# One weight read in full rows, in the last head group of the last pass

## The chip, the cores and the metric

The kernel runs on one core of one Trainium2 chip. Its time is device microseconds of one execution. Before the change the median of three runs is 1935.85 us (1933.0 to 1936.69). One further execution was profiled.

The engines are named as in the profile: PE multiplies matrices, DVE (VectorE) and ACT (ScalarE) work on vectors, POOL issues the stores, SP issues the loads.

## The reference

Forward and backward pass of four layers for one token: attention, feed-forward, attention, feed-forward, where both attention layers share the weights wq and wo and the K and V caches, and both feed-forward layers share w1 and w2.

```python
def _A_ref(x, k_cache, v_cache, wq, wo):
    q = (x @ wq).reshape(B, Sq, Hq, Dh).transpose(0, 2, 1, 3)
    k = jnp.repeat(k_cache, rep, axis=1)
    v = jnp.repeat(v_cache, rep, axis=1)
    scores = jnp.einsum("bhqd,bhkd->bhqk", q, k) * (Dh ** -0.5)
    p = _softmax(scores, axis=-1)
    o = jnp.einsum("bhqk,bhkd->bhqd", p, v)
    return o.transpose(0, 2, 1, 3).reshape(B, Sq, Hq * Dh) @ wo
...
x = x + _A_ref(_layernorm(x, axis=-1), A_k_cache, A_v_cache, A_wq, A_wo)
x = x + _B_ref(_layernorm(x, axis=-1), B_w1, B_b1, B_w2, B_b2)
x = x + _A_ref(_layernorm(x, axis=-1), A_k_cache, A_v_cache, A_wq, A_wo)
x = x + _B_ref(_layernorm(x, axis=-1), B_w1, B_b1, B_w2, B_b2)
```

The outputs are the result and the gradients of the input x, both caches, wq, wo, w1, b1, w2 and b2. The model width is 1024; there are 32 query heads of 128 columns, four K/V head groups (eight query heads each) and 65536 cached positions, all in bf16. A cache is 67 MB, wq is 1024 x 4096 (8 MB).

What the change touches is the gradient of the first layer's normalised input, which needs wq times the gradient of the queries: for each of the 1024 rows of wq, a sum over all 4096 columns of wq times dq. One head group owns 1024 of these columns.

## The kernel before, in words

The kernel passes four times over the caches. The last pass (`attn_bwd4`, called at L2024) does the backward of both attention layers at once: it reads K and V and writes dK and dV. It takes the four head groups one after another, and within a group 64 items of eight 128-position chunks each. Four items are a block: one load of K (1 MB), one of V, one store of dK and one of dV.

**Steps.** `pipeline` (L846) runs over steps; in each step every stage (`vT`, `vS`, `eT`, `dV8`, `xT`, `dK8`, `k8`) handles one item, each with its own lag. After the stages of a step, `bg.step` lets the background work go on by one piece. `Background` (L783) has an urgent list, whose first generator is asked in each step and uses up the step unless it yields "wait"; otherwise the normal list may do one piece, when it is behind an even share (L803). `bg.drain` (L826) runs all that is left. The last pass stands under no order written by hand: a scheduler arranges the instructions of each engine, and each engine then works strictly in that order.

**Memory slots.** An arena of 20 slots of 8 KB per partition (1 MB each) holds loaded blocks and outgoing blocks. In the last pass (`take_one`, L298) the free slots are of two kinds: those in the set RING, for outgoing blocks (`fill=True`), and the others, for loads. Either kind gives its oldest slot first. RING begins with up to five slots, and as each group ends, the two slots that held its softmax weights join it (`E_done`, L903). A slot is free for its next user once the program has issued its last use; the engine that uses it next waits until that use, or that store, has finished. All loads stand in SP's queue in one order, all stores in POOL's.

**The wq work.** When the last block of a group is done, `on4` (L1997) adds two pieces of background: `g_dn` (L998), urgent, for the product with the group's columns of wq, and `gwq` (L1994), normal, for the outer products that make this group's columns of the wq gradient (out_4). `g_dn` loads the group's 1024 columns in two loads of 1 MB (`wq_slabs`, L483: rows of 2 KB, four 128-row chunks each), the second when the first is used up, into load slots. It spreads the group's dq over all partitions (`g_bcast_vec`, L556), and for each of the eight row chunks DVE multiplies (L595) and ACT sums up along the row (L584). The last group is done apart: two loads of 1 MB 20 steps before the end (`pre_load`), eight chunks turned by PE (L688) and kept turned (`Rows`, L609) in `fill4` ten steps before the end, and then, when the last dq is there, one matrix product each (L722). `Rows()` takes two slots for the turned chunks (L619).

In `fill4` the rest of the normal background is drained; `g_outer_last` (L1515) then makes the last group's outer products.

Of the kernel before, what the change touches and what calls it, by code (L numbers as in the profile page):

```python
# [10 lines left out]
BF = mybir.dt.bfloat16  # L11
F32 = mybir.dt.float32
ACTF = mybir.ActivationFunctionType
ALU = mybir.AluOpType
AX = mybir.AxisListType
PSUM = bass.MemoryType.PSUM
P = 128
# [3 lines left out]
def kernel(  # L21
# [24 lines left out]
    nc = tc.nc  # L46
    D = A_x.shape[-1]
    G = A_k_cache.shape[1]
# [3 lines left out]
    HQ = QD // DH  # L52
    R = HQ // G
    F = B_w1.shape[1]
    DC, FC = D // P, F // P
# [19 lines left out]
    vec = ctx.enter_context(tc.tile_pool(name="vec", bufs=1))  # L75
    tmp = ctx.enter_context(tc.tile_pool(name="tmp", bufs=2))
    ktpool = ctx.enter_context(tc.tile_pool(name="ktpool", bufs=4))
    mvs = ctx.enter_context(tc.tile_pool(name="mvs", bufs=2))
# [15 lines left out]
    def ps_gg():  # L94
        return PS["pool"].tile([P, 1024], F32, name="ps_gg", tag="gg", bufs=2)
# [4 lines left out]
    def ps_mv(shape, dtype=F32):  # L100
        if PS["pass4"]:
            return ps_tr(shape, dtype)
        return PS["pool"].tile(shape, dtype, name="ps_mv", tag="mv", bufs=1)
# [5 lines left out]
    ident_f = const.tile([P, P], F32, name="ident_f")  # L109
    make_identity(nc, ident_f[:])  # L110
    ident_b = const.tile([P, P], BF, name="ident_b")
# [28 lines left out]
    load = {"act": 0.0, "dve": 0.0, "pe": 0.0}  # L140
# [4 lines left out]
    def add_load(act=0.0, dve=0.0, pe=0.0):  # L145
        load["act"] += act
        load["dve"] += dve
        load["pe"] += pe

    def evac(out, in_, kind="bf"):  # L150
        n = 1
        for d in in_.shape[1:]:
            n *= d
        ca = 0.17 + n * 0.00083
        cd = 0.13 + n * (0.00105 if kind == "f32" else 0.00054)

        if PS["pass4"] and kind == "bf":
            ca += 1.5
        if kind == "kta" or kind != "kt" and load["act"] + ca <= load["dve"] + cd:
            load["act"] += 0.17 + n * 0.00083  # L160
            nc.scalar.copy(out=out, in_=in_)  # L161
        else:
            load["dve"] += cd
            nc.vector.tensor_copy(out=out, in_=in_)  # L164
# [243 lines left out]
    B4_LAG = DK_LAG + J // 8  # L408
    DV_LAG = TLEAD + 1
    V_LEAD = 4 * J // 8  # L410
    ITEMS = [order_by_unit(False, SU), order_by_unit(True, SU), order_by_unit(False, HB), order_by_unit(True, J)]
# [23 lines left out]
    def rows_of(W):  # L435
        return W.rearrange("(kc p) n -> p kc n", p=P)
# [1 line left out]
    def f_rows_of(W):  # L438
        return W.rearrange("(s p j) n -> p s j n", p=P, j=4)

    def slabs(name, load, nk, kper, ncols, ahead=1, flat=False):
        pend = deque()
        ks = deque(range(0, nk, kper))

        def fetch():
            k = ks.popleft()
            i = None
            if ks and flat and NOW["wide"] and not odd_one():
                i = take_pair()
            if i is None:  # L450
                kn = min(kper, nk - k)
                sl = Slot(name)
            else:
                kn = min(2 * kper, nk - k)
                ks.popleft()
                sl = Slot(name, at=i, both=True)
            v = sl.t[:, 0:kn * ncols].rearrange("p (k n) -> p k n", n=ncols)
            nc.sync.dma_start(out=v, in_=load(k, kn))
            pend.append((k, kn, sl, v))

        def gen():
            while ks or pend:
                while ks and len(pend) < ahead:
                    fetch()
                k, kn, sl, v = pend.popleft()
                for kk in range(kn):
                    NOW["slab"] = sl
                    yield k + kk, v[:, kk, :]
                sl.over = True
                if not sl.users:  # L470
                    sl.free()
        g = gen()
        g_fetch = [fetch for _ in range(ahead)]
        return g, g_fetch
# [8 lines left out]
    def wq_slabs(g, ahead=1):  # L483
        v = rows_of(A_wq)
        return slabs("s_wq", lambda k, kn: v[:, k:k + kn, g * 1024:(g + 1) * 1024], DC, 4, 1024, ahead, True)
# [88 lines left out]
    def g_rowdots(slab_it, nk, vcol, nj, finish, name):  # L574
        n = nj * P
        y = vec.tile([P, nk], F32, name=name)
        nc.gpsimd.memset(y[:], 0.0)
        vbc = None
        due = None
        steps = 8 if PS["pass4"] else WAIT_STEPS  # L580

        def total(t, kc):
            def f():
                nc.scalar.activation(out=t[:, :], in_=t[:, :], func=ACTF.Copy, accum_out=y[:, kc:kc + 1])  # L584
            return f
        for kc, slab in slab_it:
            if vbc is None:
                vbc = yield from g_bcast_vec(vcol, nj)
                for _ in range(steps - WAIT_STEPS + 1):
                    yield "wait"  # L590
            elif kc % 4 == 0:
                for _ in range(steps):
                    yield "wait"
            t = mvs.tile([P, n], BF, name="mv_t", tag="mv_t", bufs=2)
            nc.vector.tensor_tensor(out=t[:, :], in0=slab, in1=vbc[:, :], op=ALU.mult)  # L595
            add_load(dve=0.1 + n * 0.00054, act=0.42 + n * 0.00083)
            if due is not None:
                due()
            due = total(t, kc)
            yield  # L600
        due()
        yield
        r = finish(y[:, :])
        if r is not None:
            yield from r
        yield


    class Rows:  # L609
        def __init__(self, pool=None, bufs=NWT):  # L610
            self.pool, self.bufs = pool, bufs
            self.views = deque()
            self.n = 0
            self.made = 0
            self.parts = 0
            if pool is None:

                for _ in range(2):
                    t = Slot("s_wt").t[:, :].rearrange("p (v a b) -> p v a b", v=4, a=8)  # L619
                    self.views.extend(t[:, v, :, :] for v in range(4))  # L620
                self.bufs = 8
            self.queue = deque()
            self.jobs = deque()
            self.feed = None
# [290 lines left out]
    def gsl(g):  # L915
        return slice(g * R, (g + 1) * R)
# [73 lines left out]
    def dn_finish(dn, first):  # L990
        def fin(y):
            if first:
                nc.vector.tensor_copy(out=dn[:], in_=y)
            else:
                nc.vector.tensor_tensor(out=dn[:], in0=dn[:], in1=y, op=ALU.add)
        return fin

    def g_dn(L, dn, g, first):  # L998
        yield from g_rowdots(wq_slabs(g)[0], DC, L["dqT"][:, gsl(g)], R, dn_finish(dn, first), "%s_dn%d" % (L["name"], g))


    ACT_KT = (3, 13, 15)
# [591 lines left out]
    L1, L3 = new_layer("L1", 0), new_layer("L3", 1)  # L1594
# [31 lines left out]
    lastg = [ITEMS[p][-1][0] for p in range(4)]  # L1626
    firstg = [ITEMS[p][0][0] for p in range(4)]
    PRE = {}

    def pre_load(key, pair):  # L1630
        def f():
            PRE[key] = prefetch(pair())
        return f

    gxbc = bcast_vec(gx[:], DC)
    bg = Background()
# [18 lines left out]
    rows = Rows(DENSE["pool"])  # L1655
# [20 lines left out]
    bg = Background()  # L1676
# [86 lines left out]
    rows = Rows(DENSE["pool"])  # L1763
    wo3b = wo_slabs(firstg[2])
    eps4 = root_ready(L3, lastg[1])
    ahead = [0]
# [17 lines left out]
    with tc.manual_schedule(engines=ORDERED):  # L1784
# [28 lines left out]
        job = rows.job(R, DC, lambda: dx3[:], dO_finish(L3, firstg[2]))  # L1813
# [28 lines left out]
    bg = Background()  # L1842
# [17 lines left out]
    rows = Rows(DENSE["pool"])  # L1860
# [110 lines left out]
    b4 = ExitStack()  # L1971
# [22 lines left out]
    def gwq(g):  # L1994
        return g_outer(bgpool, out_4, DC, R, [L3["n"], L1["n"]], [L3["dqT"][:, gsl(g)], L1["dqT"][:, gsl(g)]], c0=g * 1024)

    def on4(g):  # L1997
        if g != lastg[3]:
            bg.add(g_dn(L1, dn1, g, g == firstg[3]))
            bg.normal.append(gwq(g))  # L2000
        else:
            next(PRE["gwq"])
            PRE["rows"].run()
            next(PRE["gwq"])
            dxn1 = ln_bwd(dn1[:], L1["n"], L1["rstd"])
            dx0 = tmp.tile([P, DC], F32, name="dx0")
            nc.vector.tensor_tensor(out=dx0[:], in0=dx1[:], in1=dxn1[:], op=ALU.add)
            col_to_dram(dx0, D, out_1.rearrange("a b d -> (a b d)"))
            run(PRE["gwq"])
# [4 lines left out]
            kv8("v", g, c8)  # L2014

    def fill4():
        PRE["rows"] = Rows()
        PRE["rows"].add(PRE["wq4"], DC, R, lambda: L1["dqT"][:, gsl(lastg[3])], dn_finish(dn1, False))
        PRE["rows"].fill()
        bg.drain()  # L2020
        PRE["gwq"] = g_outer_last(bgpool, out_4, [L3["n"], L1["n"]], [L3["dqT"][:, gsl(lastg[3])], L1["dqT"][:, gsl(lastg[3])]],
                                  lastg[3] * 1024)
        next(PRE["gwq"])
    attn_bwd4(3, L1, L3, on4, bg, b4, [(12 + B4_LAG, last_v), (20, pre_load("wq4", lambda: wq_slabs(lastg[3], 2))), (10, fill4)])  # L2024
    b4.close()
    ps4_stack.close()

# [29 lines left out]
```

## Time and profile before

| what | value |
|---|---|
| time, median of three runs | 1935.85 us |
| profiled execution: time, span | 1936.17 us, 1934.3 us |
| DMA: moved, mean rate over the span | 787.62 MB, 407 GB/s |
| busy share of the span: PE, DVE, ACT | 81%, 61%, 54% |
| loads in the last pass: K, V, wq (1 MB each) | 64, 57, 8 |
| stores of 1 MB in the last pass | 149 |

The span runs from the first to the last instruction of the profile; the time has 1.87 us more around it. The DMA row of the page gives the busy share of the 16 DMA engines in 40 slices of 48.4 us; the last pass fills slices 25 to 40. A line with several stages gives, for each stretch, the busy time of each engine with the number of instructions, then the granted clock of PE, the DMA share and the rate. A bracket behind an instruction tells how long its engine stood idle before it, and what it waited for; a DMA wait that the profile could not place is written "issue".

### The profile page before, as it was taken

The numbers are of one execution on the slowest core, as the hardware profiler recorded it, in microseconds if no ns is written. First come the engines' busy times: TensorE is split into PE (matmuls) and PEld (weight loads), VectorE is DVE, ScalarE is ACT, GpSimd is POOL, SyncE is SP. The second block draws the span as 40 slices with busy tenths as digits, with TensorE's granted clock in tenths as the row PEclk, the third lists the DMA queues.
The fourth block names the chain that finished last, engine by engine and source line by source line (L and its number), as shares of the span: only waits on it lengthen the run. The fifth ranks groups of instructions, "written<-read, shape, count | busy, mean of one in ns | idle before, by whom it ended". The sixth has DMA issues, their size and how long they took to land. (4 is left out here: it accounts for less than half of the span.)

```text
span 1934.3 us, 66768 instructions
## 1 busy us (share of the span) xinstructions
PE 1576.4 (81%) x30099; PEld 1292.1 (67%) x30099; DVE 1172.2 (61%) x2448; ACT 1043.8 (54%) x1619; POOL 142.4 (7%) x325
## 2 busy tenths in 40 slices
PE   6878778678878878978787878888996987787977
PEld 6878777678777878867677875555654554454544
DVE  5645555255555554645464576777876886676766
ACT  3434334245333535446363465766876785576765
POOL 0000000000000000000000002111211211121211
PEclk9989999799999988998999999898988998798997
DMA  9999999999999999999999997999999999899998
GB/s 393 427 427 424 429 428 416 399 420 412 428 425 428 428 422 330 379 425 429 426 420 426 405 348 298 425 420 387 424 424 413 420 425 423 349 423 397 425 422 321
DMA packets 107148, 787.62 MB, mean 407 GB/s; under 512 B 9440, under 2 KB 16622, under 8 KB 42222
## 3 DMA queue, kind: packets, MB, share of 16 engines
q1 hardware_dynamic: 82782, 617.65, 77.3%
q0 software_dynamic: 24080, 165.70, 20.5%
q8 instruction: 235, 3.85, 0.7%
q14 instruction: 51, 0.42, 0.1%
HBM read 617.62 MB, written 165.69 MB: 405 GB/s over the span
## 5 line engine op out<-in xcount | busy, mean ns | idle before, releaser
L164 DVE COPY kt<-ps_tr 128x1024 bf16<-128x1024 bf16 x736 | 505.8, 688 | 427.1 <-PE ps_tr L1030 239.5
L161 ACT CAST arena<-ps_gg 128x1024 bf16<-128x1024 f32 x457 | 444.2, 1011 | 183.2 <-PE ps_gg L1434 132.4
L1030 PE MATMUL ps_tr<-ident_b,arena 128*128 128x128 bf16 x3840 | 308.4, 225 | 48.0 <-DMA arena<-in_A_k_cache_dram 35.3
L161 ACT COPY kt<-ps_tr 128x1024 bf16<-128x1024 bf16 x180 | 188.6, 1054 | 184.5 <-PE ps_tr L1224 107.2
L164 DVE CAST arena<-ps_gg 128x1024 bf16<-128x1024 f32 (+2 forms) x186 | 222.4, 1196 | 80.1 <-PE ps_gg L1434 36.0
L1030 PEld LDWEIGHTS <-arena 128*128 128x128 bf16 x3840 | 231.8, 101 | 56.7 <-DMA arena<-in_A_k_cache_dram 37.8
L1434 PE MATMUL ps_gg<-GG,xt 64*128 64x512 bf16 x1024 | 209.8, 408 | 51.2 <-DVE arena L164 36.7
L1131 PE MATMUL ps_acc<-arena 128*128 128x64 bf16 (+4 forms) x4096 | 204.6, 197 | 46.1 <-DMA arena<-in_A_v_cache_dram 33.7
L1048 PE MATMUL ps_sc<-L_qpad,kt 128*128 128x64 bf16 (+7 forms) x3584 | 182.6, 194 | 23.1 <-issue 11.7
L1353 PE MATMUL ps_tr<-ident_b,arena 128*128 128x128 bf16 x1824 | 178.1, 232 | 28.5 <-DMA arena<-in_A_v_cache_dram 25.7
L1113 ACT ACTIVATE arena<-S_sb,L_negm 128x128 bf16<-128x128 f32 x256 | 165.3, 1006 | 57.2 <-DVE L_negm L1098 43.6
L1224 PE MATMUL ps_tr<-ident_b,arena 128*128 128x128 bf16 x2032 | 161.7, 224 | 40.6 <-DMA arena<-in_A_v_cache_dram 39.1
L1131 PEld LDWEIGHTS <-arena 128*128 128x128 bf16 x4096 | 160.0, 101 | 52.1 <-DMA arena<-in_A_v_cache_dram 37.7
L1353 PEld LDWEIGHTS <-arena 128*128 128x128 bf16 x1824 | 117.6, 103 | 84.7 <-issue 54.2
L1048 PEld LDWEIGHTS <-kt 128*128 128x128 bf16 x3584 | 152.0, 100 | 27.3 <-issue 12.8
L1224 PEld LDWEIGHTS <-arena 128*128 128x128 bf16 x2032 | 122.6, 100 | 46.0 <-DMA arena<-in_A_v_cache_dram 41.7
L1465 PEld LDWEIGHTS <-arena 128*128 128x128 bf16 x2048 | 92.4, 101 | 56.4 <-issue 38.5
L1434 PEld LDWEIGHTS <-xt 64*128 64x128 bf16 x1024 | 64.4, 94 | 97.8 <-issue 60.2
L1113 ACT ACTIVATION_READ_ACCUMULATOR arena<-S_sb,L_negm 128x1 f32 x256 | 128.2, 501 | 0.0
L584 ACT ACTIVATE mv_t<-mv_t 128x1024 bf16<-128x1024 bf16 x96 | 102.0, 1064 | 43.0 <-DVE mv_t L595 42.8
L1278 PE MATMUL ps_acc<-dsT,arena 128*128 128x64 bf16 (+7 forms) x2048 | 102.4, 194 | 12.4 <-DMA arena<-in_A_k_cache_dram 7.2
L1390 PE MATMUL ps_sc<-DOB,kt 128*128 128x64 bf16 (+3 forms) x1824 | 112.3, 197 | 0.1
(319 smaller groups left out, 2104.3 us busy)
## 6 DMA issues: line engine op xcount, KB each, us to landing
arena<-in_A_k_cache_dram SPq DMA_DIRECT2D x82, 2048.0 KB, 21.3
arena<-in_A_v_cache_dram SPq DMA_DIRECT2D x79, 2048.0 KB, 20.1
out_dram<-arena POOLq DMA_DIRECT2D x149, 1024.0 KB, 15.6
arena<-in_A_v_cache_dram SPq DMA_DIRECT2D x84, 1024.0 KB, 13.1
arena<-in_A_k_cache_dram SPq DMA_DIRECT2D x84, 1024.0 KB, 14.6
arena<-in_A_wo_dram SPq DMA_DIRECT2D x22, 1024.0 KB, 14.9
arena<-in_B_w_dram SPq DMA_DIRECT2D x21, 1024.0 KB, 10.0
arena<-in_A_wq_dram SPq DMA_DIRECT2D x18, 1024.0 KB, 13.4
```

The lines of the kernel that those rows point to most:

```text
L161: nc.scalar.copy(out=out, in_=in_)
L164: nc.vector.tensor_copy(out=out, in_=in_)
L584: nc.scalar.activation(out=t[:, :], in_=t[:, :], func=ACTF.Copy, accum_out=y[:, kc:kc + 1])
L1030: nc.tensor.transpose(pt[:, i, :], kb8[:, i, :], ident_b[:, :])
L1048: nc.tensor.matmul(state["ps_s"][:, s:s + w, :].rearrange("p a b -> p (a b)"), lhsT=kt[:, i, :], rhs=L["qpad"][:, g, 0:w, :].rearrange("p ...
L1113: nc.scalar.activation(out=E(p, g, c0, SU)[:, :, h], in_=S[:, h, :], func=ACTF.Exp, bias=L["negm"][:, g, su, h:h + 1], scale=SCALE, accum_ ...
L1131: nc.tensor.matmul(ps_o[:, 0:w, :], lhsT=vb8[:, i, :], rhs=E(p, g, c, w), start=(c % SU == 0), stop=(c % SU == SU - 1), skip_group_check=True)
L1224: nc.tensor.transpose(pt[:, i, :], vb8[:, i, :], ident_b[:, :])
L1278: nc.tensor.matmul(ps_dq[:, 0:w, :].rearrange("p a b -> p (a b)"), lhsT=kb8[:, i, :], rhs=dsT[:, s:s + w, :].rearrange("p a b -> p (a b)") ...
L1353: nc.tensor.transpose(pt[:, i, :], vb8[:, i, :], ident_b[:, :])
L1390: nc.tensor.matmul(state["ps_dp"][:, s:s + w, :].rearrange("p a b -> p (a b)"), lhsT=vt[:, i, :], rhs=DOB[:, g, 0:w, :].rearrange("p a b - ...
L1434: nc.tensor.matmul(pg[:, 512 * h:512 * h + 512], lhsT=xt[64 * h:64 * h + 64, j1 // 8 + m, :], rhs=gg[64 * h:64 * h + 64, :, :].rearrange(" ...
```

## The change

wq is no longer read group by group in the second, third and last group's time. One generator, `g_dn_rows`, is added to the urgent background when the third group to be worked on is done, that is, at the beginning of the last group. It reads wq in eight loads of 1 MB, each 128 full rows of 8 KB. For each of these it multiplies and sums the columns of the three finished groups (three products on DVE, three sums on ACT), and has PE turn the columns of the last group, which are kept turned until the last dq is there. After each slab it lets two steps pass. The slabs, the spread dq of three groups and the two slots for turned chunks are taken from RING (the new argument `ring` of `slabs`, and `Slot("s_wt", True)`); a slab is fetched when the one before the previous one is used up. `fill4` no longer loads or turns anything.

```diff
-    def slabs(name, load, nk, kper, ncols, ahead=1, flat=False):
+    def slabs(name, load, nk, kper, ncols, ahead=1, flat=False, ring=False):
...
-                sl = Slot(name)
+                sl = Slot(name, ring)
...
-                    t = Slot("s_wt").t[:, :].rearrange("p (v a b) -> p v a b", v=4, a=8)
+                    t = Slot("s_wt", True).t[:, :].rearrange("p (v a b) -> p v a b", v=4, a=8)
...
+    def g_dn_rows(L, dn, last, rows, job):
+        rest = (G - 1) * R
+        lo = 0 if last else 1
+        v = rows_of(A_wq)
+        it, fetch = slabs("s_wq", lambda k, kn: v[:, k:k + kn, :], DC, 1, HQ * P, 2, False, True)
+        fetch[0]()
+        vsl = Slot("wq_vbc", True)
+        vb = vsl.t[:, 0:rest * P]
+        pt = ps_mv([rest, P], F32)
+        nc.tensor.transpose(pt[:, :], L["dqT"][:, lo * R:lo * R + rest], ident_f[:, :])
+        vr = tmp.tile([32, P], BF, name="bc_rows")
+        nc.vector.tensor_copy(out=vr[0:rest, :], in_=pt[:, :])
+        yield
+        for j0 in range(0, rest, 4):
+            pg = ps_gg()
+            for jj in range(4):
+                nc.tensor.matmul(pg[:, jj * P:(jj + 1) * P], lhsT=ident_b[0:rest, j0 + jj:j0 + jj + 1].to_broadcast([rest, P]),
+                                 rhs=vr[0:rest, :], start=True, stop=True)
+            evac(vb[:, j0 * P:(j0 + 4) * P], pg[:, 0:512], kind="f32")
+            if j0 % 8:
+                yield
+        y = vec.tile([P, DC, G - 1], F32, name=L["name"] + "_dny")
+        nc.gpsimd.memset(y[:, :, :], 0.0)
+        due = None
...
+        for kc, slab in it:
+            for n in range(G - 1):
+                t = mvs.tile([P, R * P], BF, name="mv_t", tag="mv_t", bufs=2)
+                nc.vector.tensor_tensor(out=t[:, :], in0=slab[:, (lo * R + n * R) * P:(lo * R + n * R + R) * P],
+                                        in1=vb[:, n * R * P:(n + 1) * R * P], op=ALU.mult)
+                add_load(dve=0.1 + R * P * 0.00054, act=0.42 + R * P * 0.00083)
+                if due is not None:
+                    due()
+                due = total(t, kc, n)
+                yield
+            rows.tra(job, kc, slab[:, last * R * P:(last + 1) * R * P], 0)
+            yield
+            if kc < DC - 1:
+                yield "wait"
+                yield "wait"
+        due()
+        yield
+        nc.vector.tensor_reduce(out=dn[:], in_=y[:, :, :], axis=AX.X, op=ALU.add)
+        vsl.free()
+        yield
...
+    beforeg = ITEMS[3][2 * len(ITEMS[3]) // G][0]
+
     def on4(g):
         if g != lastg[3]:
-            bg.add(g_dn(L1, dn1, g, g == firstg[3]))
             bg.normal.append(gwq(g))
+            if g == beforeg:
+                PRE["rows"] = Rows()
+                job = PRE["rows"].job(DC, R, lambda: L1["dqT"][:, gsl(lastg[3])], dn_finish(dn1, False))
+                bg.add(g_dn_rows(L1, dn1, lastg[3], PRE["rows"], job))
...
     def fill4():
-        PRE["rows"] = Rows()
-        PRE["rows"].add(PRE["wq4"], DC, R, lambda: L1["dqT"][:, gsl(lastg[3])], dn_finish(dn1, False))
-        PRE["rows"].fill()
         bg.drain()
...
-    attn_bwd4(3, L1, L3, on4, bg, b4, [(12 + B4_LAG, last_v), (20, pre_load("wq4", lambda: wq_slabs(lastg[3], 2))), (10, fill4)])
+    attn_bwd4(3, L1, L3, on4, bg, b4, [(12 + B4_LAG, last_v), (10, fill4)])
```

`total` (left out above) returns the ACT sum of one product; it is issued behind the next product.

More of the change, by code (lines that the diff above doesn't have):

```diff
@@ L999, in g_dn, with total, f @@
         yield from g_rowdots(wq_slabs(g)[0], DC, L["dqT"][:, gsl(g)], R, dn_finish(dn, first), "%s_dn%d" % (L["name"], g))
+    def g_dn_rows(L, dn, last, rows, job):
[22 more added lines that the diff above has]
+        due = None
+        def total(t, kc, n):
+            def f():
+                nc.scalar.activation(out=t[:, :], in_=t[:, :], func=ACTF.Copy, accum_out=y[:, kc, n:n + 1])
+            return f
+        for kc, slab in it:
[18 more added lines that the diff above has]
+        yield
     ACT_KT = (3, 13, 15)
```

## The prediction, made before the changed kernel was run

> **What bounds the kernel now.** I read the summary of the page first, then stretches of the last pass (10 us each), then what ended the idle time of VectorE (DVE), then how long transfers take from issue to landing.
>
> ```profile
> span 1934.3 us, 66768 instructions
> ...
> DMA  9999999999999999999999997999999999899998
> ```
>
> The reader sees a kernel that moves bytes: the DMA row holds 9s from end to end. In the last pass (about 1195 us to the end) a full stretch moves 422 to 428 GB/s; I use 424. What can be won there is time in which the DMA engines fall idle. The stretches (columns: busy time of PE, PE loads, DVE, ACT, POOL with counts, granted clock, DMA share, GB/s) show where:
>
> ```profile
> 1470.00:1480.00 10.00, 1.36 (x23) 1.09 (x20) 1.27 (x3) 1.23 (x3) 0.44 (x2) 0.71 1.02 425
> ...
> 1490.00:1500.00 10.00, 8.86 (x139) 6.00 (x135) 9.32 (x21) 9.52 (x14) 1.70 (x4) 1.00 0.94 355
> ...
> 1650.00:1660.00 10.00, 5.98 (x88) 3.84 (x86) 3.56 (x6) 5.01 (x7) 1.06 (x2) 0.93 1.02 419
> 1660.00:1670.00 10.00, 0.00 (x0) 0.00 (x0) 1.80 (x3) 1.08 (x3) 0.00 (x0) 0.50 0.66 277
> 1670.00:1680.00 10.00, 9.92 (x103) 6.42 (x103) 7.00 (x13) 6.66 (x11) 2.15 (x5) 0.55 0.71 269
> 1680.00:1690.00 10.00, 9.84 (x136) 6.55 (x138) 9.39 (x18) 8.58 (x10) 1.09 (x2) 1.00 0.99 367
> ...
> 1770.00:1780.00 10.00, 7.00 (x72) 4.77 (x71) 6.98 (x12) 6.45 (x9) 1.07 (x2) 0.60 0.87 305
> ```
>
> Against 424 GB/s the four rows around 1495 and 1660 to 1690 lose 1.6 + 3.5 + 3.7 + 1.3 = 10.1 us, and the row at 1770 loses 2.8 us; 1470 to 1480 loses nothing although all engines stand still. The DVE rows name the cause:
>
> ```profile
> 1478.73 0.69 DVE L595 TENSOR_TENSOR mv_t<-arena,vbc 128x1024 bf16<-128x1024 bf16 x1 [10.22 <-DMA arena<-in_A_wq_dram]
> ...
> 1668.20 0.69 DVE L595 TENSOR_TENSOR mv_t<-arena,vbc 128x1024 bf16<-128x1024 bf16 x1 [14.40 <-issue]
> ...
> 1771.05 0.69 DVE L595 TENSOR_TENSOR mv_t<-arena,vbc 128x1024 bf16<-128x1024 bf16 x1 [12.99 <-issue]
> ```
>
> L595 is the product of a wq slab in the background work of a finished head group. DVE works in order, so a late slab stops it, and PE behind it (idle 9.7, 13.6 and 12.2 us at the same places). All three are second halves of a group's wq: issued by SP at 1448.65, 1649.64 and 1750.06, used 30.1, 18.6 and 21.0 us later. Landing times over the last pass (last column, us), and below them those right after the long stall:
>
> ```profile
> out_dram<-arena POOLq DMA_DIRECT2D x149, 1024.0 KB, 15.6
> arena<-in_A_k_cache_dram SPq DMA_DIRECT2D x64, 1024.0 KB, 15.4
> arena<-in_A_v_cache_dram SPq DMA_DIRECT2D x57, 1024.0 KB, 11.7
> arena<-in_A_wq_dram SPq DMA_DIRECT2D x8, 1024.0 KB, 23.4
> ```
>
> ```profile
> out_dram<-arena POOLq DMA_DIRECT2D x3, 1024.0 KB, 6.0
> arena<-in_A_k_cache_dram SPq DMA_DIRECT2D x2, 1024.0 KB, 5.0
> ```
>
> So a 1 MB transfer takes 5 to 6 us when the queues have run dry and 12 to 23 us when they are full.
>
> ```profile
> 1885.00:1897.00 12.00, 11.92 (x98) 6.59 (x99) 6.92 (x9) 5.13 (x6) 0.53 (x1) 0.50 0.96 399
> ```
>
> After a stall of 9.5 us the granted clock is 0.50 for 12 us: 98 matmuls, where 1700 to 1730 does 132 per 10 us.
>
> **The change part by part.** The sum is made against the profiled execution: span 1934.3 us, 1936.17 us with what lies around it (1.9); the median shown is 1935.85, 0.3 below it.
>
> *Removed in the second and third group.* Four 1 MB wq loads, 16 products on DVE (0.68 us each) and 16 sums on ACT (1.06 + 0.20 us) leave the stretch 1415 to 1685. The bytes come back later, so they win nothing; the idle time caused by the two waits goes: -10.1 us. What is late next there is K and V (PE waited 10.0 us for V at 1621 with the DMA share at 1.01: no loss). The wait at 1771 in the last group belongs to a load that no longer exists: -2.8 us, replaced below. Sum -12.9 us.
>
> *Row length.* wq now comes in 8 KB rows instead of 2 KB. The 10 us stretches with a wq load move 417 to 420 GB/s, about 5 below the rest, 0.12 us per load, eight loads: -1.0 us (ends 0 and -1.5).
>
> *Work that only moves.* Products stay 24, sums 24, the transposed broadcast 24 matmuls and six evictions: 0 in total. Sixteen products and sums now fall into the last group (11 us of DVE, 20 of ACT over 10.5 blocks). Cover: DVE and ACT are 70 to 80% busy there while DMA is at 1.01; in exchange the outer products (two L161/L164 evictions in six steps instead of four) are pushed back. I cost it at 0; with the cover gone it is 31 us less about 11 pushed-back evictions of 1.1 us, shared by two engines: 9.5 us.
>
> *Added: a chain for each wq row slab.* Before, a wq slab took a load slot, free once PE had read it. Now it takes a ring slot, and SP must wait until the store that left this slot has landed. So each slab costs store landing + load landing between the issue of that store and the first product on DVE. How much work lies between comes from the order in which the built program stands: about 305 instructions of all engines a block of four items, and a block takes 10.5 us where nothing stalls (spacing of the L1411 products at 1819 to 1872), so 0.0344 us each. From store to first product the eight slabs have 936, 877, 659, 466, 348, 325, 404, 346 instructions = 32.2, 30.2, 22.7, 16.0, 12.0, 11.2, 13.9, 11.9 us. The method can be tried on the kernel before: the slot of the slab used at 1668 came free 161 instructions (5.5 us) ahead, the load took 18.6, which gives a wait of 13.1 (seen: 14.40); at 1771: 289 instructions, 9.9 us, 21.0, so 11.1 (seen: 12.99).
> The landing pair is bounded by the rows above: dry 6.0 + 5.0 = 11.0; full 15.6 + 13.5 (mean of K and V, whose row length wq now has) = 29.1. Each stall lets queues run down, so neither end lasts: I take the middle, 10.8 + 9.3 = 20.1. Waits of the eight: 0, 0, 0, 4.1, 8.1, 8.9, 6.2, 8.2 = 35.5 us. Part of it the transfers need anyway: slabs stand 386 instructions (13.3 us) apart, 1.26 blocks, which move 5.3 MB of K, V, dK, dV, 1.05 of wq and 0.3 of outer products = 6.7 MB, 15.7 us at 424; 2.4 us for each of five = 12.0. Net +23.5 us. At the dry end the net is 0; at the full end the waits are 86.9 less 14.4 = +72.5. The half clock after each stall shortens the next wait by as much as it slows the work between, so it adds 0 (the end above: 5 x 3.6 us, from 98 matmuls in 12 us against 132 in 10).
>
> *What queues behind the added wait.* On SP, 2, 4, 3, 4, 2, 3 and 3 K and V loads stand between the row loads and are held with them. Their slots now come free 9 to 12 steps ahead instead of mostly 5 to 9, since wq leaves the load slots: 0; without that cover a K load late as at 1885 costs 9.5 us. On POOL three out_4 stores stand ahead of the last two out_2 stores.
>
> *The end.* The urgent work takes 52 steps of the last group, so 12 units of outer products are left to the drain, where 1 was: eight more evictions (1.0 to 1.2 us) and three row builds (1.9) = 14.6 us over two engines, +7.3. The turning of the last wq (eight evictions, 6.2 us) leaves the end: -3.1. K loads, no longer kept out by four wq slots, are not late at 1876 to 1885, which saves the idle DMA of the half-clock stretch: -2.0. Sum +2.2. The 2 MB of later stores (4.9 us) fit into a share of 0.7 after 1915.
>
> Sum: 1934.3 - 12.9 - 1.0 + 23.5 + 2.2 = 1946.1; + 1.9 = 1948.0 for this execution, 1947.7 against the median.
>
> *Two pages beside it.* The Trainium skill, "TensorE: Matmul & The Clock Gate" (Part 1: The HAM clock gate), has the array at half rate after an idle window of about 3.4 us, until some 3.4 us of sustained work. The trace agrees on the half, not on the way back: 12 us. By the page five stalls would cost 5 x 1.7 = 8.5 us where the rows give 18, and the sum takes neither.
>
> **The rivals.**
> 1. *The chain runs dry (faster).* If store and load land in 6.0 and 5.0 us, 11.0 is below all eight distances, no product waits, and only the gains stay: 1934.3 - 12.9 - 1.0 + 2.2 = 1922.6, 1924.2 with the surroundings. For it: the landing times at 1655 to 1690. Against: these followed a 14.4 us stall; at 1800 to 1880 a store took 23.2 us. It decides below a pair of about 13 us.
> The Trainium skill, "DMA: Bandwidth & Descriptors" (Queues, rings and completion order), says that each DMA engine takes turns between the queues that have work, so a store need not stand behind the loads; that speaks for this rival. No run here shows the turns.
> 2. *It cancels.* With a pair of 16 us the last five waits are 0, 4.0, 4.8, 2.1 and 4.1 = 15.0, less 2.4 for each of four: +5.4. With half of the lost cover (4.8) that is 1924.2 + 10.2 - 0.3 = 1934.1, within 0.2%. For and against it: the same two landing times, between which it lies.
> 3. *The chain stays full (much slower).* +72.5: 1997. Against: in that case DMA would be a third idle, and idle queues are not full.
>
> **How the numbers follow.** Forecast (slower by the chain) 0.54, its own range 1940 to 1980; rival 1 0.28; rival 2 0.14; rival 3 0.04. 0.2% is 3.9 us, about what can be told from no change. Faster 0.28, same 0.14, slower 0.58. Leaving out one in ten on each side, the range goes from below rival 1 to inside the full end: 1919 to 1978.
>
> **What the profile after would show.** Right: no DVE idle over 5 us on a wq product before about 1700; the last group's first block ahead by 10 to 20 us; then four to six DVE idles of 4 to 10 us before the row products (L1033), with SP waiting at L458 on out_dram, the clock at 0.5 to 0.8 and DMA share at 0.8 to 0.95. Wrong: row products that never wait (rival 1), or idle DMA in the second and third group in spite of the missing loads, or an end from block 64 that is longer by over 5 us.

## The result, and the profile after

The changed kernel takes 1955.0 us (median) against 1936.0 us for the kernel before: ratio 1.0097, 95% interval 1.0080 to 1.0114. It is slower, as forecast (1947.7, range 1919 to 1978), by 19 us where 11.8 were forecast. The profiled execution has a span of 1953.8 us (before 1934.3).

The summary of the page shows no change of kind: DMA stays the row of 9s, with a weaker last digit.

```profile
span 1953.8 us, 66829 instructions
...
DMA  9999999999999999999999988999999999999995
```

The 10 us stretches of the last pass, to be read against those of before (columns: busy time of PE, PE loads, DVE, ACT, POOL with counts, granted clock, DMA share, GB/s):

```profile
1490.00:1500.00 10.00, 9.71 (x126) 5.94 (x123) 8.08 (x11) 7.91 (x10) 2.29 (x4) 1.00 1.02 423
1660.00:1670.00 10.00, 7.78 (x101) 4.88 (x99) 4.99 (x9) 7.01 (x8) 1.78 (x5) 1.00 1.02 426
1670.00:1680.00 10.00, 8.53 (x86) 4.86 (x85) 6.55 (x9) 5.06 (x5) 1.43 (x3) 0.66 1.01 425
1680.00:1690.00 10.00, 9.15 (x132) 5.86 (x131) 7.11 (x13) 6.89 (x7) 1.93 (x4) 1.00 1.02 420
1780.00:1790.00 10.00, 8.57 (x106) 5.51 (x104) 6.23 (x10) 7.05 (x10) 1.07 (x2) 0.84 1.00 376
1810.00:1820.00 10.00, 1.85 (x13) 1.09 (x13) 4.33 (x7) 3.61 (x6) 0.00 (x0) 0.51 0.89 348
1870.00:1880.00 10.00, 7.68 (x79) 4.65 (x78) 8.00 (x15) 6.91 (x9) 0.53 (x1) 0.58 0.67 282
1920.00:1930.00 10.00, 8.13 (x98) 5.09 (x99) 7.46 (x28) 5.25 (x7) 0.98 (x2) 0.81 0.52 211
1930.00:1940.00 10.00, 6.70 (x35) 1.84 (x33) 6.17 (x13) 5.58 (x7) 2.35 (x4) 0.50 0.59 247
```

The first four stretches, which moved 355, 277, 269 and 367 GB/s before, are full now: the idle DMA of the second and third group is gone. The others are what replaced it: 282 to 376 GB/s in the last group, and a long end in which the engines move 211 to 247 GB/s and PE falls to half clock (0.81, then 0.50).

To count this I use one ledger for every kernel below: in each stretch of 10 us, the time lost against 424 GB/s is 10 x (1 - GB/s / 424); the losses are added up between fixed times. All kernels but one move the same bytes, so the difference of two spans is the difference of their losses. The ledger is good to some 3 us: from 1190 to 1410 us, where the kernels stand in the same order, it gives between 5.1 and 11.4 us.

```
loss of DMA time (us)    1410-1690   1690-1900   1900-end   span
before                      10.3         5.3         9.8    1934.3
after                        0.3        25.1        20.7    1953.8
```

So the second and third group won 10.0 us, the last group lost 19.8, the end lost 10.9 (the stretch ahead of them, which the change does not touch, differs by 1.7). For the last group, the idle times of DVE ahead of the row products:

```profile
1776.13 0.69 DVE L1033 TENSOR_TENSOR mv_t<-arena 128x1024 bf16<-128x1024 bf16 x1 [8.84 <-DMA arena<-in_A_wq_dram]
...
1815.67 1.29 DVE L1033 TENSOR_TENSOR mv_t<-arena 128x1024 bf16<-128x1024 bf16 x2 [9.83 <-DMA arena<-in_A_wq_dram]
...
1870.97 0.69 DVE L1033 TENSOR_TENSOR mv_t<-arena 128x1024 bf16<-128x1024 bf16 x1 [11.24 <-DMA arena<-in_A_wq_dram]
```

and sums over 1690 to 1900 us (us in total, times, longest), first DVE's wait for a row slab, then what SP's queue stood for:

```profile
DVE mv_t L1033 <- DMA arena<-in_A_wq_dram: 36.6, 6, 11.2
```

```profile
SPq L458 <- DMA out_dram<-arena: 99.2, 8, 22.8
SPq L361 <- PE ps_acc L1515: 59.6, 7, 15.2
```

The 36.6 us over six slabs are what the forecast called 35.5 over five. SP stands 99.2 us before its eight row loads (L458), each time because the ring slot that it is to fill is still being stored. What that does to the queue shows in SP's own rows (start us, us):

```profile
1703.51 0.33 SPq L361 DMA_DIRECT2D arena<-in_A_k_cache_dram  x1
1726.92 0.33 SPq L458 DMA_DIRECT2D arena<-in_A_wq_dram  x1
1727.35 0.51 SPq L361 DMA_DIRECT2D arena<-in_A_k_cache_dram  x1
1727.95 1.14 SPq L361 DMA_DIRECT2D arena<-in_A_v_cache_dram  x1
```

From 1703.5 to 1726.9 no load is issued at all; the K and V loads follow the row load at once, so they had only stood behind it.

### The profile page after: what moved, and what is told of

The parts are those of the page before. It is cut to its first block, busy times and chain, and to the rows that moved or that the text cites. A ratio compares the mean times of both kernels' runs of the same rounds, so it can differ in the third digit from the quotient of the medians.

```text
span 1953.8 us, 66829 instructions
## 1 busy us (share of the span) xinstructions
PE 1594.9 (82%) x30097; PEld 1303.2 (67%) x30097; DVE 1172.0 (60%) x2444; ACT 1045.0 (53%) x1619; POOL 142.7 (7%) x323
## 5 line engine op out<-in xcount | busy, mean ns | idle before, releaser
L161 ACT CAST arena<-ps_gg 128x1024 bf16<-128x1024 f32 (+1 forms) x460 | 447.5, 1009 | 194.1 <-PE ps_gg L1484 118.2
L1098 PE MATMUL ps_sc<-L_qpad,kt 128*128 128x64 bf16 (+7 forms) x3584 | 182.6, 194 | 21.1 <-issue 9.9
L1098 PEld LDWEIGHTS <-kt 128*128 128x128 bf16 x3584 | 151.9, 100 | 25.4 <-issue 11.3
L1274 PEld LDWEIGHTS <-arena 128*128 128x128 bf16 x2032 | 124.8, 102 | 42.5 <-DMA arena<-in_A_v_cache_dram 37.6
L1440 PEld LDWEIGHTS <-kt 128*128 128x128 bf16 x1824 | 83.3, 102 | 39.2 <-issue 38.0
## 6 DMA issues: line engine op xcount, KB each, us to landing
arena<-in_A_k_cache_dram SPq DMA_DIRECT2D x82, 2048.0 KB, 20.8
arena<-in_A_v_cache_dram SPq DMA_DIRECT2D x79, 2048.0 KB, 21.1
arena<-in_B_w_dram SPq DMA_DIRECT2D x21, 1024.0 KB, 10.1
arena<-in_A_wq_dram SPq DMA_DIRECT2D x18, 1024.0 KB, 10.9
```

What stands on the lines that cost most here:

```text
L1098: nc.tensor.matmul(state["ps_s"][:, s:s + w, :].rearrange("p a b -> p (a b)"), lhsT=kt[:, i, :], rhs=L["qpad"][:, g, 0:w, :].rearrange("p ...
L1274: nc.tensor.transpose(pt[:, i, :], vb8[:, i, :], ident_b[:, :])
L1440: nc.tensor.matmul(state["ps_dp"][:, s:s + w, :].rearrange("p a b -> p (a b)"), lhsT=vt[:, i, :], rhs=DOB[:, g, 0:w, :].rearrange("p a b - ...
```

## The experiments

The theory on record: the row slabs cost what they cost because a ring slot must wait for its store, then for its load, and DVE, PE and ACT stand in order behind the late slab. Rivals: long rows that cost the transfers themselves; the row work itself; the end. Each kernel is timed beside the kernel before, and ratios are to it. "The end" is the time from the last X product on DVE (block 64) to the last instruction: 31.1 us before, 41.4 after.

**Slots without a store in the chain (own3).**

```
+ own = deque(Slot("s_wq", True) for _ in range(3))
- slabs("s_wq", ..., DC, 1, HQ * P, 2, False, True)
+ slabs("s_wq", ..., DC, 1, HQ * P, 3, False, True, own)   # fetch: sl = own[0]; own.rotate(-1)
```

> Changed kernel, but the eight row slabs go in turn through three slots that they keep to themselves (taken from the ring once, given back after the last slab), three slabs ahead. From the second round on no slab waits for a store. Chain theory (a slab's slot waits for the store that left it): the three DVE idles of 8.8, 9.8 and 11.2 us before L1033 go, SP stands at L458 on out_dram for under 40 us in all (99.2 in the changed kernel), and the time falls by 20 to 25 us to 1930 to 1936. Rival, rows of 8 KB cost the transfers themselves: loads stay above 42 us of DMA-engine time per MB in the last group (38 elsewhere) and the time stays at 1950 to 1956. In both cases the stretch from block 64 to the end stays near 41 us, since 12 units are still left to the drain.

Measured: ratio 1.0068 (1.0047 to 1.0088), 1950.9 us; the end 42.7 us. SP's waits in 1690 to 1900 us, and what PE waited for at the broadcast:

```profile
SPq L361 <- PE ps_acc L1520: 105.5, 12, 16.1
...
SPq L460 <- PE ps_tr L690: 28.8, 4, 14.8
SPq L460 <- DMA out_dram<-arena: 25.2, 3, 20.8
```

```profile
1737.12 0.58 PE L1020 MATMUL ps_gg<-bc_rows,ident_b 24*128 24x128 bf16 x4 [10.55 <-ACT arena L161]
```

The stand for stores fell from 99.2 to 25.2 us as expected, but DVE still waits 26.5 us for row slabs (36.6 before the edit). In place of the store SP now stands for K's slots, which PE frees (105.5 us, 59.6 in the changed kernel). That stand is no cost in itself, for the kernel before has the same in these 210 us, at nearly the full rate:

```profile
SPq L361 <- PE ps_acc L1465: 105.3, 13, 13.0
```

New are 28.8 us for its own three slots, which PE still turns, with the other loads behind; a row load issued at 1758.4 was used 26.6 us later. A new wait came as well: the slot of the broadcast vector (`wq_vbc`) is taken from the ring after the three slabs, its store had not landed, and PE, behind ACT's eviction into it, stood 10.6 us. My theory predicted 1930 to 1936 and fails in this form: with three quarters of the stand for stores gone, the slabs are still late. (The 4 us are hardly more than the two intervals leave open.) The time is inside what the rival of long rows had forecast (1950 to 1956); that rival is taken up under loadshare.

**More lead, same slots (ahead3).**

```
- slabs("s_wq", ..., DC, 1, HQ * P, 2, False, True)
+ slabs("s_wq", ..., DC, 1, HQ * P, 3, False, True)
```

> Changed kernel, with three row slabs ahead instead of two, ring slots as they come. Each load is issued about 13 us earlier in the order, but its slot still waits for a store. If the cost is DVE's wait for the late slab, the waits before L1033 fall below 2 us each and the time goes to 1935 to 1940. If the cost is SP standing still for the store's landing, with the K and V loads behind it, SP still stands for 80 to 110 us on out_dram, PE waits for K or V instead, and the time stays within 5 us of 1955.

Measured: 1.0054 (1.0035 to 1.0074), 1947.7 us, between the two forecasts.

```profile
SPq L458 <- DMA out_dram<-arena: 91.3, 8, 20.3
```

```profile
DVE mv_t L1033 <- DMA arena<-in_A_wq_dram: 28.7, 3, 11.4
```

SP stands almost as long, and DVE waits 28.7 us in three waits instead of 36.6 in six. The loss in 1690 to 1830 us is the same (16.1 against 15.8), and falls from 9.3 to 3.7 in 1830 to 1900. A third slab in flight helps late, not where the waits begin.

**Outer products beside the row work (share).**

```
                 due = total(t, kc, n)
-                yield
+                yield "wait"
             rows.tra(job, kc, slab[:, last * R * P:(last + 1) * R * P], 0)
-            yield
+            yield "wait"
```

> Changed kernel, but each step of the row work lets one step of the outer products run beside it (the plain yields become waits), so that they are no longer pushed to the drain. If the long end (41 us from block 64, 31 in the kernel before) comes from the 12 units left to the drain: it falls to 31 to 34 us and the time to 1945 to 1949, the waits before L1033 staying. If the end is long for other reasons, or the units cost as much wherever they are: 1952 to 1958.

Measured: 1.0054 (1.0035 to 1.0073), 1947.8 us. The end falls by 12.8 us, from 41.4 to 28.6; block 64 comes 5.6 us later (1918.0 against 1912.4), which leaves 7.2. After block 64 there are 14 evictions from `ps_gg` into slots and three row builds fewer (17 and three against 31 and six). The long end was the outer products that the row work had pushed to the drain. This shows why they cost so much there; ACT's and PE's rows in the end of the changed kernel (start, us, idle before and what ended it):

```profile
1941.33 1.01 ACT L161 CAST arena<-ps_gg 128x1024 bf16<-128x1024 f32 x1 [0.71 <-PE ps_gg L1562]
1943.05 1.01 ACT L161 CAST arena<-ps_gg 128x1024 bf16<-128x1024 f32 x1 [0.70 <-PE ps_gg L1562]
```

```profile
1943.25 0.62 PE L1562 MATMUL ps_gg<-rowb,rowa 2*128 2x512 bf16 x2 [0.24 <-DVE arena L164]
1944.11 0.62 PE L1562 MATMUL ps_gg<-rowb,rowa 2*128 2x512 bf16 x2 [0.24 <-ACT arena L161]
```

ACT makes one eviction of 1.01 us each 1.72 us, DVE one of 1.22 us each 1.93 us, and each waits for PE; but PE waits too. `ps_gg` has two buffers (L95): PE fills one only when its last eviction is done, and the engine that evicts it waits for that. Eviction, 0.62 us of matmuls and two handovers of together 0.09 us make up both periods, so neither engine is busy throughout and two engines do not halve the time. The half clock is about 0.2 us of a period: at 1804, at full clock, the same two matmuls took 0.41 us.

**The kernel before with both halves of wq fetched at once (b_ahead2).**

```
- g_rowdots(wq_slabs(g)[0], DC, L["dqT"][:, gsl(g)], ...)
+ g_rowdots(wq_slabs(g, 2)[0], DC, L["dqT"][:, gsl(g)], ...)
```

> Kernel before, with both 1 MB halves of a group's wq fetched at once in the three groups' background products (two ahead instead of one), nothing else. If the DVE waits of 10.2, 14.4 and 13.0 us for the second half are what the change wins in the second and third group: these waits go and the time falls by 10 to 13 us to 1923 to 1926. If two load slots held for longer only make K and V late: DMA still idle somewhere in 1440 to 1800, 1934 to 1945.

Measured: 1.0054 (1.0034 to 1.0074), 1946.9 us, slower. The waits for the second half are gone but for one idle of 3.5 us before L595, and V is late in their place (39.6 us in 1410 to 1690, in five waits):

```profile
1625.83 1.03 PE L1353 MATMUL ps_tr<-ident_b,arena 128*128 128x128 bf16 x8 [10.68 <-DMA arena<-in_A_v_cache_dram]
...
1647.68 1.03 PE L1353 MATMUL ps_tr<-ident_b,arena 128*128 128x128 bf16 x8 [10.78 <-DMA arena<-in_A_v_cache_dram]
```

The loss in 1410 to 1690 is 13.7 us (10.3 before). The slot that waits longer with wq in it is a slot that K or V lacks.

**One row slab for all eight rounds (noload).**

```
- slabs("s_wq", ..., DC, 1, HQ * P, 2, False, True)
+ slabs("s_wq", ..., 1, 1, HQ * P, 1, False, True)
- for kc, slab in it:
+ slab = next(it)[1]
+ for kc in range(DC):
```

> Changed kernel, but only the first of the eight row slabs is loaded; all eight rounds of products, sums and turning use it again (seven loads of 1.05 MB and their waits are left out, so the result dx0 is another). The bytes alone are 7.3 MB, 17.3 us at 424 GB/s: if the row work on DVE and ACT is what slows the last group, 1936 to 1940. If the loads cost more than their bytes (SP standing for slots, DVE for slabs, K and V behind them): the stretch 1690 to 1900 loses under 8 us of DMA time against 25.1 in the changed kernel, and the time is 1917 to 1925. The end from block 64 stays near 41 us in both.

Measured: 0.9913 (0.9888 to 0.9939), 1919.4 us. That is 35.6 us below the changed kernel, 17.3 for the bytes and 18.3 on top. Three stretches of the last group:

```profile
1780.00:1790.00 10.00, 9.67 (x140) 6.32 (x138) 9.98 (x19) 9.13 (x12) 2.72 (x4) 1.00 1.01 422
1790.00:1800.00 10.00, 9.43 (x128) 6.15 (x124) 9.91 (x16) 10.00 (x16) 2.68 (x5) 1.00 1.02 426
1810.00:1820.00 10.00, 9.45 (x147) 6.13 (x145) 9.51 (x16) 8.93 (x13) 1.64 (x3) 1.00 1.01 422
```

With all the row work in place DVE is busy to 95% and more, and DMA moves 422 to 426 GB/s: the loss from 1690 to 1830 is 3.0 us (15.8 in the changed kernel). From 1690 to 1900, the stretch of the forecast, it is 20.3 and not under 8, since this shorter run has 25 us of its end in there; up to block 64 (1874.5) it is 7.0, where the changed kernel loses 25.2 up to its block 64 and the kernel before 5.5. So the moved products and sums cost nothing that the ledger can tell, and the loads cost 18 us more than their bytes. The end stays, 42.3 us.

**Row slabs in load slots (loadslot).**

```
- slabs("s_wq", ..., DC, 1, HQ * P, 2, False, True)
+ slabs("s_wq", ..., DC, 1, HQ * P, 2, False, False)
```

> Changed kernel with the row slabs in load slots, as wq had them before, instead of ring slots. SP no longer stands for a store before a row load. If the store in the chain is the cost: 1933 to 1942. If a slab's cost is the slot that it takes, whichever kind (load slots are then short, and K and V late, as when the kernel before fetches both halves at once): PE waits for K or V by 5 to 11 us several times in the last group and the time is 1950 to 1965.

Measured: 1.0046 (1.0032 to 1.0059), 1945.0 us: 10 us below the changed kernel. DVE's idle time before the row products falls from 36.6 to 9.8 us (one part of it the profile could not place), and PE's waits for V rise from nothing:

```profile
DVE mv_t L1033 <- issue: 5.8, 1, 5.8
DVE mv_t L1033 <- DMA arena<-in_A_wq_dram: 4.0, 1, 4.0
```

```profile
PE ps_tr L1403 <- DMA arena<-in_A_v_cache_dram: 13.4, 3, 8.1
```

The kind of slot is worth 10 us net. The loss in 1690 to 1900 is 14.1 (25.1 before the edit), the end 42.2.

**The kernel before with both halves in ring slots (b_ring2).**

```
- g_rowdots(wq_slabs(g)[0], ...)
+ g_rowdots(wq_slabs(g, 2, True)[0], ...)   # Slot(name, True)
```

> Kernel before, three groups' background products as they were, but both 1 MB halves fetched at once and in ring slots, so that K and V keep theirs. If the changed kernel's gain up to block 45 (16 us) is only the load slots that wq no longer takes in the second and third group, this has most of it without the last group's cost: 1922 to 1929. If the wait for a store's landing on SP costs here what it costs in the last group: SP stands on out_dram for over 15 us a slab, and 1934 to 1945.

Measured: 0.9988 (0.9975 to 1.0001), 1934.5 us, within what can be told from no change. K is late now, by some 11 us, near the places where the second halves were:

```profile
1651.04 0.29 PE L1465 MATMUL ps_acc<-X,arena 128*128 128x64 bf16 x2 [10.95 <-DMA arena<-in_A_k_cache_dram]
...
1747.43 0.28 PE L1465 MATMUL ps_acc<-X,arena 128*128 128x64 bf16 x2 [11.49 <-DMA arena<-in_A_k_cache_dram]
```

SP stands 46.3 us for stores before the row loads in 1410 to 1800, at most 14.0 at once. The loss in 1410 to 1690 stays at 9.9 us. Neither kind of slot recovers it while the loads stand in those groups; in every variant of the changed kernel it is 0.0 to 1.3 us.

**Lead and outer products together (ahead3share).** Both edits from above.

> Changed kernel with both edits: three row slabs ahead and outer products beside the row work. Alone they won 7.3 and 7.2 us, in different stretches (1830 to 1900, and after block 64). If the stretches are independent: 1939 to 1942. If the outer products that come back take the time that the lead had won: 1945 to 1949.

Measured: 0.9987 (0.9972 to 1.0002), 1934.5 us: 20.5 us below the changed kernel, where the two alone won 7.3 and 7.2. Neither forecast had this. SP stands 74.3 us for stores, DVE waits 15.4 us for slabs, the end is 26.6 us. Why the sum is more than its parts was not isolated.

**Load slots and outer products together (loadshare).** Both edits from above.

> Changed kernel with the row slabs in load slots (two ahead) and outer products beside the row work. Alone they won about 10 and 7 us. Sum, if independent: 1937 to 1939. If the second one wins more where the loads come in time, as it did with three slabs ahead (20.5 us together, 14.5 as a sum): 1930 to 1934, below the kernel before. If the outer products take up what the load slots had won: 1942 to 1946.

Measured: 0.9966 (0.9952 to 0.9980), 1930.5 us. This is faster than the kernel before, as the second forecast had it. The end is 25.7 us; SP stands for no store in the last group. Four stretches in it (columns as above), and DVE's one idle time before a row product and PE's wait for K in 1690 to 1900:

```profile
1780.00:1790.00 10.00, 9.37 (x155) 6.66 (x154) 9.63 (x17) 8.85 (x11) 2.40 (x4) 1.00 1.01 422
1790.00:1800.00 10.00, 9.22 (x131) 6.14 (x128) 9.61 (x21) 9.00 (x13) 1.68 (x3) 1.00 1.01 424
1820.00:1830.00 10.00, 9.04 (x125) 5.90 (x123) 9.77 (x19) 9.49 (x14) 1.61 (x3) 1.00 1.02 425
1830.00:1840.00 10.00, 7.05 (x102) 4.66 (x101) 6.12 (x12) 6.69 (x9) 1.92 (x4) 0.95 1.01 424
```

```profile
DVE mv_t L1033 <- issue: 3.9, 1, 3.9
```

```profile
PE ps_acc L1515 <- DMA arena<-in_A_k_cache_dram: 14.3, 4, 6.3
```

In each of the four stretches a row slab is issued in 8 KB rows, DMA moves its full rate, and the load queue takes 37.9 to 38.0 us of engine time a MB, where that rival had over 42: long rows cost nothing, and the rival is out.

**A third load slot (load3share).** `ahead` 3 instead of 2 in loadshare.

> The same with three row slabs ahead, in load slots. If what is left of the waits (5.8 and 4.0 us before L1033) is a lead too short: 4 to 8 us below the one with two ahead. If a third load slot is then missing for K and V: PE waits of 5 us and more for K or V in 1740 to 1900, and 0 to 10 us above it.

Measured: 1.0014 (1.0000 to 1.0027), 1941.1 us, 10.6 above it. PE's waits:

```profile
PE ps_acc L1515 <- DMA arena<-in_A_k_cache_dram: 20.2, 5, 7.6
...
PE ps_tr L1403 <- DMA arena<-in_A_v_cache_dram: 6.8, 2, 5.5
```

27.0 us instead of 15.2 for K and V: the third slot is missing there, as the second forecast had it (the time is 0.6 us above its range).

**First slab in a load slot, seven in the ring (mixshare).** `Slot(name, k > 0)` in ahead3share.

> Three slabs ahead and outer products beside the row work, the first slab in a load slot and the other seven in ring slots (with all eight in ring slots this took 1934.5 us). If SP's stand of 22.8 us before the first row load, with K and V behind it, costs the 4.9 us that DMA loses in 1690 to 1760: 1929 to 1932. If the second and third slab only stand there in its place: 1933 to 1936.

Measured: 0.9985 (0.9972 to 0.9998), 1934.9 us, as with all eight in the ring (1934.5). The loss in 1690 to 1760 is 6.0 us against 4.9; SP's longest stand for a store is 29.4 us instead of 22.8. The stand only moved to the next slab.

**Two more slots for the loads (loadplanes).**

```
  def E_done(g, c0, n):
-     RING.add(plane(lay, g))
+     if g != beforeg: RING.add(plane(lay, g))     # in loadshare
```

> Row slabs in load slots, two ahead, outer products beside the row work (1930.5 us), and the two slots of the third head group's exponentials, when they come free early in the last group, go to the loads instead of the stores' ring: what the row slabs take from K and V is given back. If slots for K and V are what is left (PE waits of 5.7 and 6.3 us for K): 1922 to 1927. If the ring then runs short instead (evictions waiting for out_dram) or something else bounds the last group: 1929 to 1936.

Measured: 0.9995 (0.9984 to 1.0007), 1936.7 us, 6 us above loadshare. K, V and the row slabs are never late here (no such wait in 1690 to 1900), but the ring runs short:

```profile
1750.61 0.58 PE L1018 MATMUL ps_gg<-bc_rows,ident_b 24*128 24x128 bf16 x4 [10.40 <-ACT arena L161]
```

This is the broadcast of own3 again, behind an eviction on ACT; what ACT waited for, 12.99 us, the profile writes as "issue" here, where in own3 it was a store. In all, evictions wait 31.8 us for stores in 1690 to 1900, against 14.6 in loadshare. In these variants slots are scarce on both sides: whichever side got one, the other waited. That this sets the whole order of the times is not shown.

```
last group and end (us)  ratio   SP on    DVE on   PE on   loss 1690   the
                                 stores   wq       K, V    to 1900     end
after                    1.0097   99.2     36.6     5.6      25.1      41.4
own3                     1.0068   25.2     26.5     0        18.5      42.7
ahead3                   1.0054   91.3     28.7     3.1      19.8      42.2
share                    1.0054  104.5     33.5     0        22.1      28.6
loadslot                 1.0046    0        9.8    16.1      14.1      42.2
ahead3share              0.9987   74.3     15.4     4.3      14.9      26.6
mixshare                 0.9985   75.9      8.3    10.9      13.3      25.3
loadshare                0.9966    0        3.9    15.2      12.1      25.7
load3share               1.0014    0        0      27.0      19.5      27.4
loadplanes               0.9995    0        0       0        17.5      25.2
```

The waits, losses and ends are those of the profiled execution, which lies 2.8 and 2.6 us below the median in own3 and mixshare, 2.4 and 6.0 above it in load3share and loadplanes. "DVE on wq" includes the idle times of 5.8 and 3.9 us that the profile writes as "issue". SP's stand for stores does not order the times: it is 74.3 us at 0.9987 and 25.2 us at 1.0068.

## Why the prediction was right, and where not

*Idle DMA in the second and third group, -10.1 us.* Right: -10.0 by the ledger, and it stays so in all variants. The last group's first block came 8.1 us ahead (1713.4 against 1721.5), a little less than the 10 to 20 given.

*The chain in the last group.* The size was right: waits of 36.6 us where the sum had 35.5, mean landing of the eight row loads 10.1 us where it took 9.3, median landing of the stores issued in 1690 to 1900 12.1 us where it took 10.8, net loss 19.8 us where the terms -2.8, +23.5 and the -2.0 for K gave +18.7. The distribution was not: slabs 3, 5 and 8 waited 8.8, 9.8 and 11.2 us, where five similar waits from the fourth on were forecast. So part of the closeness is luck, and the mechanism was half of the truth. Load slots instead of ring slots took 10 us away, which is what the ring slots cost net; but own3, which has a quarter of the stand for stores left, won 4 us, and its slabs were late all the same. That the row loads cost 18.3 us beyond their bytes is shown (noload); that all of it is the store is refuted.

*Queueing of K and V on SP, 0.* The hold is there (23.4 us without any load at 1703 to 1727). The runs show no price for it alone: the changed kernel loses 5.1 us in 1690 to 1760, but loadslot, where SP goes at most 14.0 us without a load, loses 5.6, and own3 and noload, with holds of 20.8 and 18 us, lose 2.3 and 2.0.

*Moved work, 0, and row length, -1.0.* The first is right (noload). For the second the runs show no cost of either sign: the full rate with 8 KB rows in loadshare, where I had 417 to 420 for any stretch with a wq load; a difference of 1 us in all is below what the ledger can tell.

*The end: wrong.* From block 64 on the forecast was +7.3 - 3.1 = +4.2 (the rest of the +2.2, the -2.0 for K, lies ahead of block 64); measured +10.3, beyond the mark of 5 us that I had set. The count was right: after block 64 there are eight evictions from `ps_gg` into slots and three row builds more (31 and six against 23 and three), and the turning is gone. The step that failed is the price, "14.6 us over two engines, +7.3": the two engines do not halve the time, since each waits for PE to refill its buffer (share). There 14 evictions and three row builds, 21.1 us at the forecast's prices, were worth 12.8 and not 10.6. At that rate the 14.6 us would cost 8.9, and the turning, credited with 3.1, would have saved nothing; how the 10.3 divide between the two was not isolated. By the spans the forecast was short by 7.7 us (+19.5 against +11.8): 6.1 behind block 64, and 1.6 ahead of it.

*Half clock, 0.* The six kernels with the shorter end stand as long at half clock in 1690 to 1900 us as the changed kernel (58 to 80 us against 68, counting twice the missing share of the clock; 37.6 before), so it does not set the order among them. That it is free is not shown: in loadshare PE is busy through 1746 to 1760 at a clock of 0.50 while DMA falls to shares of 0.07 and 0.12 in between (rows below), and that kernel loses 9.5 us in 1690 to 1760.

*The rivals.* The chain that runs dry did not come, nor did the cancelling one (its sum takes the 0.3 us off twice; 1934.4 is still within 0.2%). The dry landing of 5 to 6 us leaves out V, which took 10.0 us in the same stretch of the kernel before. In the changed kernel row loads did land in 6.4 to 16.0 us, but stores issued at 1700 to 1730 took 20 to 28 us. The Trainium skill, "DMA: Bandwidth & Descriptors" (Queues, rings and completion order), has each engine take turns between the queues that have work. The runs agree: where both queues have a backlog they share evenly (2.19 MB of stores and 2.07 MB of loads in 1850 to 1860 of loadshare, landing in 19.9 and 17.3 us). That did not help the ring slots, since a store first stands behind the stores ahead of it (an argument; no run takes these away).

## What to carry to other kernels

Before moving a load to where DMA idles less, ask which pool its buffer comes from and what that pool's buffers wait for: in an in-order issue queue one load that waits for its slot holds every load behind it, and here each slot given to wq, to K and V, or to the stores was missing to another. Do not halve the price of background work that a new urgent task pushes past the last loop because two engines share it: the tail has nothing to hide it, and with two buffers each engine waits for the refill. Letting it run beside the new work, with the slabs in load slots, turned the same change from 1.0097 into 0.9966.

## What the runs showed of the hardware

A full DMA share does not mean the full rate. Load queue (q1) of the changed kernel in 1850 to 1860 us and in 1890 to 1900 us (packets, MB, share of 16 engines):

```profile
q1 hardware_dynamic: 290, 2.11, 50.0%
```

```profile
q1 hardware_dynamic: 275, 2.06, 64.1%
```

The first is 37.9 us of engine time a MB (50.0% of 160 us for 2.11 MB), the second 49.8, and that stretch moves 354 GB/s at a share of 1.00. From 1690 to 1900 us the changed kernel has 14 stretches of 21 above 40 us a MB, loadshare and the kernel before four each. What makes these loads slow was not tried; in the second stretch it is not the rows of wq, for SP issues only K there (from 1864.8 on).

The half clock can last long. In loadshare PE stood still for 3.2 us at 1726 to 1729, and then (columns as above):

```profile
1728.00:1730.00 2.00, 0.44 (x4) 0.15 (x3) 0.00 (x0) 2.00 (x3) 1.15 (x2) 0.93 0.87 369
...
1730.00:1732.00 2.00, 2.00 (x22) 1.07 (x21) 1.37 (x3) 0.81 (x1) 0.00 (x0) 0.50 1.01 425
...
1746.00:1748.00 2.00, 2.00 (x22) 1.20 (x20) 1.62 (x3) 0.82 (x1) 0.00 (x0) 0.50 0.07 29
...
1758.00:1760.00 2.00, 2.00 (x17) 1.51 (x17) 2.00 (x3) 1.01 (x1) 0.00 (x0) 0.50 0.12 49
...
1762.00:1764.00 2.00, 1.90 (x43) 1.42 (x39) 2.00 (x5) 1.52 (x3) 0.73 (x1) 1.00 0.95 295
```

30 us at 0.50, with PE busy almost throughout. The Trainium skill, "TensorE: Matmul & The Clock Gate" (Part 1: The HAM clock gate), gives about 3.4 us of sustained work for the way back; here it took 30, and 13 after the stall of 9.9 us that ended at 1818 in the changed kernel.
